# The first frequency step's rows written straight into its tile, two lead pieces, stores from ScalarE's queue

## The chip, the cores and the metric

The kernel runs on one core of a Trainium2 chip. The metric is device time in microseconds of one execution. Before the change three runs gave 1628.64 us in the median (1623.98 to 1630.26).

## The reference

The reference is a long causal convolution followed by a mixture of experts. Cut to what matters:

```python
# x, v: (4, 11456, 128); pos_emb: (11456, 64); w1: (64, 64); w2: (64, 128)
h_filt = (np.maximum(pos_emb @ w1, 0.0) @ w2) * np.exp(-0.01 * pos)[:, None]
u = x * v
Uf, Hf = np.fft.rfft(u, n=2 * S, axis=1), np.fft.rfft(h_filt, n=2 * S, axis=0)
y = np.fft.irfft(Uf * Hf[None], n=2 * S, axis=1)[:, :S]
x = (x * y).reshape(4 * 11456, 128)          # input of the second part

do_compute = x @ w_skip > 0
xc = x[do_compute]
logits = xc @ w_gate                          # 8 experts
e_idx = np.argmax(logits, axis=1)
gate_w = softmax(logits).max(-1)
y[m] = gate_w[m, None] * (np.maximum(xc[m] @ w1[e], 0.0) @ w2[e])   # m: tokens of expert e, F = 1024
out[do_compute] = xc + y
```

## The kernel before

The sequence is cut into `NB` = 3 blocks of 3840 positions, and each block is transformed in two stages, 60 x 64: a first transform over `K1` = 60 (matrix `c1`), and a second over `N2` = 64 with the twiddles folded in (`c2`, one 128x128 matrix for each of the 60 frequencies k). The 128 channels are handled in `NP` = 4 quarters of `DH` = 32.

**First phase** (`first_phase`, class `First`). For the first quarter it takes 16 data steps. A step loads 768 KB of x and v (`load`, L178, on SP's queue), multiplies them on VectorE (`mult`, L185), and transforms them in `Q` = 2 pieces: TensorE into PSUM (L202), ScalarE from PSUM to the buffer `xs` (L204), of which there are `XS` = 4. The result of a step has 120 partitions, (frequency k, real or imaginary c), and is stored to a DRAM tensor `x1d[0]` (`store`, L190, SP's queue), after the first piece of the next step. Between the pieces a generator, `filt`, computes the filter: 12 pieces of `post` (loaded on POOL's queue, L232; matmul L240; ReLU on ScalarE, L241), then 8 chunks x 3 blocks of L267 (TensorE), L268 (VectorE), L248 (TensorE) and L250 (ScalarE, into `fx`), and after each chunk two stores to the DRAM tensor `x1f` from POOL's queue (L256). `x1f` holds the filter for all quarters.

**Frequency phase** (`freq_phase`). It has 60 steps n: quarter h = n // 15, and `KS` = 4 of the 60 frequencies. `load(n)` issues on SP's queue, in this order: for h = 0 the matrices `c2` (L359), the data rows from `x1d[h]` (L362) and the filter's columns from `x1f` (L363) into a tile `x1` of [128, 4, 480], 384 columns of data and 96 of filter. The partition of `x1` is (c, n2), so a row of the first stage, which lies in one partition (k, c) for all n2, has to be spread over 64 partitions. That is what the trip through DRAM does. There are `QX` = 4 tiles `x1`, and three are loaded ahead. A step then does: L373 on TensorE (second transform into PSUM `xp`), L376 to L378 on ScalarE and L385 and L386 on VectorE (filter into `g`), L393 on VectorE (products `y`, `p1`, `p2`), L465 and L466 on POOL (sums), L404 on TensorE (transform back) with L405 on ScalarE, and the store to `zd` (L414, SP's queue). The PSUM pool `qps` for L404 and L202 has four buffers.

The data steps of the other three quarters, 48 in all, run inside the frequency phase: a generator `others()` yields after each half step, and `step()` takes two of these pieces whenever a credit allows. The first `LEAD` = 6 pieces (three data steps) are taken before the first frequency step is begun, and their products are on VectorE; later ones are on POOL.

After the last step the output phase (`out_phase`) transforms back over 60 and runs the experts.

The order of the instructions on each engine and queue is written out by hand: both phases stand under `manual_schedule`, so each engine's instructions and each queue's transfers go out in program order.

## Time and profile before

The profiled execution took 1626.78 us; its span is 1625.0 us (first to last instruction of the core), and its mean granted TensorE clock was 0.976.

| stage | from, to (us) | PE busy | ACT busy | DVE busy | POOL busy | share of the DMA engines |
|---|---|---|---|---|---|---|
| first phase, start | 0 to 40 | 28.92 | 15.93 | 6.77 | 6.88 | 0.80 |
| first phase, rest | 40 to 119 | 72.86 | 44.26 | 24.45 | 8.36 | 0.95 |
| between the phases | 119 to 143 | 8.96 | 5.16 | 2.88 | 0.00 | 0.75 |
| frequency phase with data steps | 160 to 568 | 407.65 | 204.21 | 324.92 | 354.43 | 0.97 |
| whole span | 1625.0 | 1537.8 | 794.3 | 1203.4 | 1084.8 | |

How to read the lines below: L202 is line 202 of the kernel. PE is TensorE's matmuls, PEld its weight loads, DVE VectorE, ACT ScalarE, POOL GpSimd, SP the engine that issues most transfers; a "q" behind a name (ACTq, SPq) is that engine's instruction queue, where a transfer's issue is shown with the time that the issue took, not the transfer. In a group's line stand the count, the busy time, the mean ns of one, the idle time of the engine before it and what ended that.

### The profile page before, as it was taken

How to read it: one execution, taken by the hardware profiler on the slowest of the kernel's cores; microseconds unless marked ns; L12 is line 12 of the kernel's file. 1: busy time of each engine (PE TensorE's matmuls, PEld its weight loads, DVE VectorE, ACT ScalarE, POOL GpSimd, SP SyncE). 2: the span in 40 equal slices, each digit the busy share in tenths (PEclk: the TensorE clock that was granted, in tenths of full speed). 3: DMA queues.
4: the chain of work that ended last, by engine and by line, in shares of the span. 5: the costliest groups of instructions: out<-in, count | busy, mean ns of one | idle time of the engine just before them, and what ended most of it. 6: DMA issues, size and time to landing. Idle time of an engine off the chain costs nothing.

```text
span 1625.0 us, 26505 instructions
## 1 busy us (share of the span) xinstructions
PE 1537.8 (95%) x8272; PEld 961.0 (59%) x8272; DVE 1203.4 (74%) x2424; ACT 794.3 (49%) x1677; POOL 1084.8 (67%) x850
## 2 busy tenths in 40 slices
PE   7985999999999999996789999999989999999997
PEld 2552444444444444442347766666767888888997
DVE  1324877888788799993877777777887777777886
ACT  4552455444544544442235544544345655556774
POOL 1112988888888878870156647855677888867885
PEclk9996999999999999997889999999999999999999
DMA  7998999999999799968978768877631111111110
GB/s 283 333 339 315 379 377 377 356 329 335 321 343 338 255 265 316 312 160 295 301 222 255 229 214 257 255 223 240 209 87 33 47 45 47 45 37 37 38 36 23
DMA packets 198532, 361.92 MB, mean 223 GB/s; under 512 B 64650, under 2 KB 138778, under 8 KB 198350
## 3 DMA queue, kind: packets, MB, share of 16 engines
q1 hardware_dynamic: 181078, 320.12, 58.9%
q0 software_dynamic: 16704, 38.89, 8.5%
q8 instruction: 67, 1.10, 0.3%
q10 hardware_dynamic: 608, 1.20, 0.2%
q14 instruction: 75, 0.61, 0.1%
HBM read 216.96 MB, written 145.69 MB: 223 GB/s over the span
## 4 chain that ended last, share of the span: by engine, by line
PE 84%; DMA 6%; DVE 5%; issue 3%; POOL 1%; ACT 1%; SPq 0%; DVEq 0%; ACTq 0%; POOLq 0%
PE ps L404 20%; PE xp L373 12%; PE bank L782 6%; PE y L1018 5%; PE ps L202 5%; PE my L834 4%; PE my L832 4%; PE hp L700 4%; PE my L833 4%; PE hp L702 4%; PE hp L701 4%; PE mh L700 2%; PE tp L1031 2%; PE mh L702 1%; PE mh L701 1%
## 5 line engine op out<-in xcount | busy, mean ns | idle before, releaser
L404 PE MATMUL ps<-y,c 128*128 128x512 f32 x720 | 331.3, 597 | 0.3
L465 POOL TENSOR_TENSOR y<-y,p 128x2048 f32<-128x2048 f32 x59 | 267.7, 4537 | 68.8 <-DVE p L393 68.8
L706 POOL DMA_INDIRECT out<-o,ids x186 | 199.9, 1075 | 123.3 <-DVE o L713 87.0
L404 PEld LDWEIGHTS ps<-y,c 128*128 128x128 f32 x720 | 133.4, 190 | 173.0 <-issue 155.9
L637 POOL DMA_INDIRECT xt<-out,ids x186 | 193.1, 1038 | 49.3 <-issue 30.6
L393 DVE TENSOR_TENSOR p<-xp,g 128x1024 f32<-128x1024 f32 x240 | 217.4, 947 | 0.0
L393 DVE TENSOR_TENSOR y<-xp,g 128x1536 f32<-128x1536 f32 x120 | 210.8, 1757 | 4.1
L821 DVE SCALAR_TENSOR_TENSOR hh<-hp,hh 128x1024 fp32r<-128x1024 f32 x130 | 158.4, 1219 | 68.3 <-ACT hh L820 68.1
L405 ACT COPY z<-ps 128x512 f32<-128x512 f32 x180 | 105.6, 586 | 176.5 <-PE ps L404 167.5
L820 ACT ACTIVATE hh<-hp 128x1024 fp32r<-128x1024 f32 x130 | 134.2, 1032 | 75.4 <-PE hp L702 75.4
L589 POOL DMA_INDIRECT lists<-pl,lies x32 | 53.6, 1676 | 141.0 <-DVE step L1116 72.3
L466 POOL TENSOR_TENSOR y<-y,p 128x1024 f32<-128x1024 f32 x59 | 139.0, 2356 | 4.6
L677 DVE TENSOR_TENSOR ws<-wf,ws 128x1024 fp32r<-128x1024 f32 x104 | 126.7, 1219 | 15.5 <-ACT ws L672 12.1
L610 POOL MEMSET idle<- 128x512 f16 x248 | 134.6, 543 | 0.2
L1018 PE MATMUL y<-zt,c 128*64 128x512 f32 x384 | 114.1, 653 | 19.8 <-DMA zt<-zd 11.2
L700 PE MATMUL hp<-hl,ws 128*128 128x512 f32 (+1 forms) x344 | 123.3, 359 | 3.5 <-DVE tb L626 1.9
L202 PE MATMUL ps<-wf,c 60*120 60x384 f32 x512 | 111.8, 532 | 14.8 <-DVE wf L185 14.3
L782 PEld LDWEIGHTS bank<-wd,h 128*128 128x128 f32 x896 | 104.2, 191 | 31.5 <-issue 31.4
L373 PE MATMUL xp<-x,wf 128*128 128x480 f32 x256 | 115.5, 575 | 7.3 <-issue 3.6
L204 ACT COPY wf<-ps 120x384 f32<-120x384 f32 x256 | 105.5, 493 | 29.5 <-PE ps L202 28.9
L702 PE MATMUL hp<-hl,ws 128*128 128x512 f32 (+1 forms) x344 | 116.4, 338 | 0.0
L834 PE MATMUL my<-hh,ws 128*128 128x512 f32 (+1 forms) x344 | 116.3, 338 | 0.0
(162 smaller groups left out, 3062.1 us busy)
## 6 DMA issues: line engine op xcount, KB each, us to landing
wf<-xv SPq DMA_DIRECT2D x64, 768.0 KB
zt<-zd SPq DMA_DIRECT2D x64, 768.0 KB
x1d<-wf SPq DMA_DIRECT2D x64, 720.0 KB
x<-x1d SPq DMA_DIRECT2D x60, 768.0 KB
zd<-z SPq DMA_DIRECT2D x118, 384.0 KB
out<-xm SPq DMA_DIRECT2D x96, 258.0 KB
ox<-xo SPq DMA_DIRECT2D x96, 256.0 KB
x1f<-fx POOLq DMA_DIRECT2D x16, 720.0 KB
```

Source lines behind the costliest of these rows:

```text
L202: nc.tensor.matmul(ps[p], self.c1[rows], u[rows, q * RUN:(q + 1) * RUN], start=True, stop=True)
L373: nc.tensor.matmul(xp[:, k, 0:(NS + NB) * DH], c2(n % PER * KS + j * KH + k), x1[:, j * KH + k], start=True, stop=True)
L393: nc.vector.tensor_tensor(o[:, :, :, j * KH:(j + 1) * KH].rearrange("p s a k b d -> p (s a) k b d"), x[:, None].broadcast_to([128, m, KH, ...
L404: nc.tensor.matmul(zps, c3[:, a, :], y[:, blk, a], start=(a == 0), stop=(a == 1))
L465: nc.gpsimd.tensor_tensor(y[:, 1:], y[:, 1:], p1, ALU.add)
L637: ins = nc.gpsimd.indirect_dma_start(out=xt[:, j], out_offset=None, in_=self.rows[0:have], in_offset=bass.IndirectOffsetOnAxis(ap=ids[:, j ...
L700: nc.tensor.matmul(hp, w[:, 0, c], hl[:, 0], start=True, stop=False)
L702: nc.tensor.matmul(hp, w[:, 1, c], hl[:, 0], start=False, stop=True)
L706: ins = nc.gpsimd.indirect_dma_start(out=self.rows, out_offset=bass.IndirectOffsetOnAxis(ap=ids[:, j:j + 1], axis=0), in_=o, in_offset=Non ...
L782: nc.tensor.matmul(bank[:, j * D:(j + 1) * D], h[f][:, j * 128:(j + 1) * 128], wd[s][:, f * D:(f + 1) * D], start=(f == 0), stop=(f == F / ...
L834: nc.tensor.matmul(y, w2[:, 1, c], h[:, 0], start=False, stop=(f == F // 128 - 1))
L1018: nc.tensor.matmul(y[p * 64:(p + 1) * 64], c4s[ch // C4][:, ch % C4, p, :], z[:, NP * p:NP * (p + 1)], start=True, stop=True)
```

## The change

- `First` takes the pool of the `x1` tiles and allocates one tile at once, `head`. A new function `direct` copies rows of the first stage from their SBUF partition to the partitions (c, n2) of `head`: for each of the 4 frequencies of the first step and each c one transfer of four rows. `data` calls it in every step of the first quarter (rows of 384 columns, 1.5 KB), `filt` for both halves of each chunk (rows of 96 columns, 384 B), all on ScalarE's queue. `load(0)` returns `head` and reads nothing from `x1d` and `x1f`.
- The first 8 of the 120 partitions are no longer stored to `x1d[0]`, so that store has 112 partitions. The `x1f` store is cut into 112 and 8 partitions.
- `store` issues on ScalarE's queue, at the end of the step itself.
- `LEAD` goes from 6 to 2: one data step is taken ahead of the first frequency step, and its product alone is on VectorE.
- The loads of x and v for later data steps are held back in the first phase (17 in place of 19 are issued there) and go out behind the loads for frequency step 1.
- `post` is loaded from SP's queue, one more piece ahead, and each load is issued behind the matmul of its turn.
- The credit of `step()` is spread over one more iteration. The pool of the `x1` tiles is opened earlier and closed after the frequency phase.

```diff
--- before.py
+++ after.py
@@ -42,7 +44,7 @@
 SOON = 4
 NKNOWN = sum(n * u for c, n, u in KNOWN)
 NEARLY = sum(n * u for c, n, u in KNOWN[:SOON])
-LEAD = 6
+LEAD = 2
 FLEAD = 2
 FEND = 2
 KS = 4
@@ -151,8 +153,9 @@
     ALL = NP * STEPS
     XV, US, XS = 3, 2, 4
 
-    def __init__(self, nc, i, x1d, x1f, mc, stage):
+    def __init__(self, nc, i, x1d, x1f, mc, stage, qx):
         self.nc, self.i, self.x1d, self.x1f = nc, i, x1d, x1f
+        self.qx, self.head = qx, self.tile(qx)
         n = self.Q * self.RUN
         at = [0]
 
@@ -167,9 +170,20 @@
         nc.sync.dma_start(self.c1, i["c1"])
         self.loaded, self.late = 0, []
 
-    def ahead(self, step):
-
-        while self.loaded < min(step + self.XV, self.ALL):
+    @staticmethod
+    def tile(qx):
+        return qx.tile([128, KS, (NS + NB) * DH], F32, name="x1")
+
+    def direct(self, eng, xs, n, cols):
+
+        for k in range(KS):
+            for c in range(2):
+                at = c * N2 + n
+                eng.dma_start(self.head[at:at + xs.shape[1], k, cols], xs[2 * k + c:2 * k + c + 1])
+
+    def ahead(self, step, most=XV):
+
+        while self.loaded < min(step + most, self.ALL if step >= self.STEPS else self.STEPS + LEAD // self.Q):
             self.load(self.loaded)
             self.loaded += 1
 
@@ -187,7 +201,7 @@
     def store(self):
 
         for dst, xs in self.late:
-            self.nc.sync.dma_start(dst, xs)
+            self.nc.scalar.dma_start(dst, xs)
         self.late = []
 
     def data(self, step, pool):
@@ -202,13 +216,14 @@
                 nc.tensor.matmul(ps[p], self.c1[rows], u[rows, q * RUN:(q + 1) * RUN], start=True, stop=True)
             for p in range(2):
                 nc.scalar.copy(xs[:, 2 * q + p], ps[p])
-            if q == 0:
-                self.store()
             if q < Q - 1:
                 yield
-        self.late.append((self.x1d[h][:, :, 2 * Q * ch:2 * Q * (ch + 1)].rearrange("k c m w -> (k c) m w"), xs))
-        if ch == self.STEPS - 1:
-            self.store()
+        n = 2 * Q * ch
+        at = KS if h == 0 else 0
+        if h == 0:
+            self.direct(nc.scalar, xs, n, slice(0, RUN))
+        self.late.append((self.x1d[h][at:, :, n:n + 2 * Q].rearrange("k c m w -> (k c) m w"), xs[2 * at:]))
+        self.store()
         yield
 
     def filt(self, fc, fp, pool):
@@ -229,15 +244,17 @@
         def positions(blk, k):
 
             pt = fp.tile([128, P], F32, name="post", bufs=4)
-            nc.gpsimd.dma_start(pt, i["post"][blk, k // P])
+            nc.sync.dma_start(pt, i["post"][blk, k // P])
             return pt
-        posts = [positions(*pc) for pc in pieces[:3]]
+        posts = [positions(*pc) for pc in pieces[:2]]
+        yield
+        posts += [positions(*pc) for pc in pieces[2:4]]
         yield
         for n, (blk, k) in enumerate(pieces):
-            if n + 3 < len(pieces):
-                posts.append(positions(*pieces[n + 3]))
             ps = pool.tile([128, P], F32, name="fa")
             nc.tensor.matmul(ps, w1, posts.pop(0), start=True, stop=True)
+            if n + 4 < len(pieces):
+                posts.append(positions(*pieces[n + 4]))
             nc.scalar.activation(hs[blk][:, k:k + P], ps, AF.Relu)
             yield
 
@@ -253,8 +270,12 @@
                 return
             for p in range(2):
                 n0 = p * H2 + ch * M
-                nc.gpsimd.dma_start(self.x1f[:, :, n0:n0 + M].rearrange("k c m w -> (k c) (m w)"),
-                                    xs[p].rearrange("k m h s d -> k (m h s d)"))
+                w = NB * DH
+                self.direct(nc.scalar, xs[p].rearrange("k m h s d -> k m (h s d)")[:, :, 0:w], n0, slice(self.RUN, self.RUN + w))
+                there = self.x1f[:, :, n0:n0 + M].rearrange("k c m w -> (k c) (m w)")
+                here = xs[p].rearrange("k m h s d -> k (m h s d)")
+                for rows in (slice(0, 112), slice(112, 2 * K1)):
+                    nc.gpsimd.dma_start(there[rows], here[rows])
         last = iter(())
         for ch in range(H2 // M):
             xs = [fp.tile([2 * K1, M, NP, NB, DH], F32, name=f"fx{p}") for p in range(2)]
@@ -285,6 +306,8 @@
         left = 0.0
         pieces = NB * 64 * H2 // 512 + 2 * NB * H2 // 4
         pace = (pieces - FLEAD) / (fi.Q * (fi.STEPS - FEND))
+        next(f)
+        fi.ahead(0, 1)
         next(f)
         fi.ahead(0)
         fi.mult(0)
@@ -318,7 +341,6 @@
         tc.manual_schedule(),
         tc.tile_pool(name="qc", bufs=1, reuse_waits="tile") as qc,
         tc.tile_pool(name="qp", bufs=2, reuse_waits="tile") as qp,
-        tc.tile_pool(name="qx", bufs=QX, reuse_waits="tile") as qx,
         tc.tile_pool(name="qpx", bufs=1, space=PSUM, reuse_waits="tile") as qpx,
         tc.tile_pool(name="qps", bufs=4, space=PSUM, reuse_waits="tile") as qps,
     ):
@@ -344,7 +366,7 @@
         def step():
 
             n = fi.STEPS * fi.Q
-            credit[0] += (n - LEAD) / (PER - QX) if done[0] < n else n / PER
+            credit[0] += (n - LEAD) / (PER - QX + 1) if done[0] < n else n / PER
             while credit[0] >= fi.Q:
                 credit[0] -= fi.Q
                 for _ in range(fi.Q):
@@ -357,7 +379,9 @@
             ks = slice(KS * k, KS * k + KS)
             if h == 0:
                 nc.sync.dma_start(c2(ks.start, KS), i["c2"][k])
-            x1 = qx.tile([128, KS, (NS + NB) * DH], F32, name="x1")
+            if n == 0:
+                return fi.head
+            x1 = fi.tile(fi.qx)
             w = NB * DH
             nc.sync.dma_start(x1[:, :, 0:fi.RUN], fi.x1d[h][ks].rearrange("k c n w -> (c n) k w"))
             nc.sync.dma_start(x1[:, :, fi.RUN:], fi.x1f[ks, :, :, h * w:(h + 1) * w].rearrange("k c n w -> (c n) k w"))
@@ -418,7 +442,11 @@
         done_z = []
         todo = others()
         ys = {}
-        xs = {n: load(n) for n in range(QX - 1)}
+        xs = {}
+        for n in range(QX - 1):
+            xs[n] = load(n)
+            if n == 1:
+                fi.ahead(fi.STEPS)
         for _ in range(LEAD):
             next(todo)
         gs, xps = {}, {}
@@ -1276,11 +1304,12 @@
     x1f = nc.dram_tensor("x1f", (K1, 2, N2, NB * D), F32).ap()
     zd = nc.dram_tensor("zd", (2, NP, H2 * 2 * K1 + ZR, NS * DH), F32).ap()
     lists = nc.dram_tensor("lists", (ROOM // PL, PL), I32).ap()
-    with tc.tile_pool(name="mc", bufs=1) as mc:
+    with tc.tile_pool(name="mc", bufs=1) as mc, ExitStack() as stack:
         wf = mc.tile([128, 2 * E * F], F32, name="wf")
-        fi = First(nc, i, x1d, x1f, mc, wf)
+        c3 = mc.tile([128, 2, 128], F32, name="c3")
+        qx = stack.enter_context(tc.tile_pool(name="qx", bufs=QX, reuse_waits="tile"))
+        fi = First(nc, i, x1d, x1f, mc, wf, qx)
         spare = wf[:, fi.used:]
-        c3 = mc.tile([128, 2, 128], F32, name="c3")
         first_phase(tc, fi)
         nc.scalar.dma_start(c3, i["c3"])
         nc.scalar.dma_start(zd.rearrange("p h r w -> (p h) r w")[:, H2 * 2 * K1:], i["none"])
@@ -1301,6 +1330,7 @@
                     yield
                 later["ex"].weights(e, 1)
         freq_phase(tc, nc, i, fi, zd, c3, spare, prepare())
+        stack.close()
         out_phase(tc, i, out, zd, later["ex"], later["consts"])
 
 
```

More of the change, by code (lines that the diff above doesn't have):

```diff
@@ L1 @@
+from contextlib import ExitStack
 import numpy as np
```

## The prediction

> **What bounds the kernel now.** I read the stages first, then the chain of waits where two of them meet, because the change acts there. The chain between the first phase and the frequency phase, in order of time (start, us, what):
>
> ```profile
> 115.44 1.30 ACT wf L204 x3
> ...
> 118.83 18.50 DMA x1d<-wf
> ...
> 137.35 0.39 SPq L362
> ...
> 138.06 4.58 DMA x<-x1f
> ...
> 142.78 2.74 PE xp L373 x3
> ```
>
> The first phase's last copy out of PSUM ends near 117, its last x1d store goes out at 118.83, and TensorE gets the first frequency step's rows at 142.78. So 24.0 us pass between that store and the first matmul of L373: 18.5 for the store to land, some for the issues, 4.6 for the load. The stages around it (busy us of each engine, granted clock, share of the DMA engines, GB/s):
>
> ```profile
> 40.00:119.00 79.00, 72.86 (x524) 42.84 (x520) 24.45 (x32) 44.26 (x96) 8.36 (x16) 0.98 0.95 335
> 119.00:143.00 24.00, 8.96 (x25) 3.88 (x26) 2.88 (x3) 5.16 (x12) 0.00 (x0) 0.51 0.75 259
> ...
> 160.00:568.00 408.00, 407.65 (x1144) 177.91 (x1143) 324.92 (x399) 204.21 (x531) 354.43 (x125) 1.00 0.97 341
> ```
>
> The columns after the length are PE, PEld, DVE, ACT, POOL. In the first phase the DMA engines are 95% busy and PE 92% (72.86 of 79); ACT works 44.26 of 79, a little over half. Between 119 and 143 PE does 8.96 us, at a clock of 0.51: this is the hole. From 160 on PE is never idle, so whatever work lands there costs its full time. All of the change lies before about 165 us or in the data steps of that last stretch.
>
> **The change part by part.**
>
> *The hole.* With the first step's rows written straight into its tile, its matmuls wait for the last of these writes, not for the round trip through DRAM. The nearest row for a small transfer from issue to release is this (chain of waits, 1 KB):
>
> ```profile
> 809.70 3.71 DMA ids<-lists
> ```
>
> So the first L373 would come 3.7 us after the last issue, in place of 24.0 us: 20.3 us is the most that can be won here, if the first phase ends when it did.
>
> *The direct writes.* They are many. `direct` issues KS x 2 = 8 transfers a call. `data` calls it in each of 16 steps (128), the filter for both halves of 8 chunks (128): 256 transfers of 6 KB or 1.5 KB, four rows each, all on ScalarE's queue. Does issuing occupy ScalarE? The timeline's first microseconds show it:
>
> ```profile
> 0.75 0.42 ACTq L224 DMA_DIRECT2D fw<-w  x1
> ...
> 1.20 0.46 ACTq L225 DMA_DIRECT2D win<-win  x1
> ...
> 1.68 0.45 ACTq L1285 DMA_DIRECT2D c<-c  x1
> 2.17 1.25 ACTq L1286 DMA_DIRECT2D zd<-none  x1
> 3.45 1.28 ACT L241 ACT_TABLE_LOAD   x1 [3.45 <-issue]
> ...
> 8.69 0.60 ACT L241 ACTIVATE h<-fa 128x512 f32<-128x512 f32 x1 [3.96 <-PE fa L240]
> ```
>
> The table load depends on nothing, yet starts at 3.45, just behind the fourth issue (2.17 + 1.25 = 3.42). An issue therefore stands in line with ScalarE's copies and takes 0.42 us or more here. Cheaper ones are on SP's queue, for small tables:
>
> ```profile
> 600.46 0.30 SPq L500 DMA_DIRECT2D shift<-shift  x1
> 600.81 0.29 SPq L502 DMA_DIRECT2D bump<-bump  x1
> 601.14 0.32 SPq L506 DMA_DIRECT2D sums<-sums  x1
> 601.50 0.32 SPq L508 DMA_DIRECT2D runs<-runs  x1
> 601.87 0.25 SPq L510 DMA_DIRECT2D lines<-lines  x1
> ```
>
> From one start to the next are 0.33 to 0.37 us. A write of four rows on ScalarE's queue isn't in the trace. Its lower bound is 0.25 us, the shortest issue above; its upper bound is 0.58, from the only other ScalarE issues:
>
> ```profile
> 731.69 1.16 ACTq L414 DMA_DIRECT2D zd<-z  x2
> ```
>
> I take 0.33, the start-to-start time of `bump`, whose eight rows are nearest to four: 256 x 0.33 = 84.5 us (64 to 148).
>
> What this is added to is ScalarE's own work up to 119 us (line, busy us, idle before):
>
> ```profile
> L204 ACT COPY wf<-ps 120x384 f32<-120x384 f32 x64 | 27.5, 495 | 10.7 <-PE ps L202 10.7
> L250 ACT COPY fx<-ps 120x512 f32<-120x512 f32 x48 | 26.8, 592 | 28.1 <-PE ps L248 14.8 <-DMA x1f<-fx 11.9 <-PE fa L267 1.3
> L241 ACT ACTIVATE h<-fa 128x512 f32<-128x512 f32 x12 | 7.2, 597 | 14.7 <-PE fa L240 14.7
> ```
>
> 61.5 us of copies, against 110 us from its first one at 8.69 to 119. There is room for some 49 us of issues, and I count 84.5. So ScalarE becomes the bound of the first phase.
>
> A rule speaks the other way. The Trainium skill, "DMA: Bandwidth & Descriptors", section "Issuing engines are not separate DMA queues", holds that issue time is usually small beside the transfer itself; by it the 84.5 would drop out of the sum and the forecast would turn into the first rival's time. Here 6 KB at the 335 GB/s of the first-phase row is 0.02 us, and the 0.33 issue is the longer of the two; the trace does not bear the rule out for such pieces.
>
> *The x1d stores on ScalarE's queue.* SP's price is
>
> ```profile
> L190 SPq DMA_DIRECT2D x1d<-wf x64: 317/388/2376, 16.8 to 565.3; - x64
> ```
>
> (minimum, median, maximum ns). In the first phase 16 x 0.39 = 6.2 us more on ScalarE. In the frequency phase 48 of them join a ScalarE that is busy 204.21 of 408 us: at the median 18.7 us, at the maximum 114 us, both less than its idle time. I cost them at 0; what covers them is the four PSUM buffers between PE and the copies. On SP they freed the loads behind them, which waited long:
>
> ```profile
> SPq L190 <- ACT wf L204: 80.2, 15, 10.9
> ...
> SPq L178 <- DMA fw<-w: 0.8, 1, 0.8
> ```
>
> (80.2 us in the first 142 us, in 15 waits.) I credit nothing for that: xv loads come sooner, but ScalarE sets the pace.
>
> *Idle time of ScalarE.* The second row above is an xv load that waits for a weight transfer whose bytes it doesn't touch; in the frequency phase there is the like:
>
> ```profile
> SPq L359 <- DMA zd<-z: 2.3, 6, 0.5
> ```
>
> A c2 load shares nothing with a zd store. I read it as a small set of completion slots given out in turn, so a burst of 16 writes (5.3 us) may wait for its own first ones to land (3.7). Besides, ScalarE waited 10.7 + 14.7 us for PE in L204 and L241, part of it at the start for `post`. Bounds 0 and 25 us; I take 12.
>
> *End of the first phase.* 8.7 (first copy) + 61.5 + 84.5 + 6.2 + 12 = 172.9, then 3.7 to land: first L373 at 176.6 in place of 142.78, **+33.8**. The lead step's copies lie inside the 3.7.
>
> *The second frequency step* still goes through DRAM. Its rows are wanted when L373 starts on it, in the profile at
>
> ```profile
> 151.69 1.85 PE L373 MATMUL xp<-x,wf 128*128 128x480 f32 x4 [3.56 <-issue]
> ```
>
> 8.9 us after the first, so at 185.5. The last store leaves at 172.9, lands some 4 us later with the DMA engines no longer full (the same traffic over 173 us), and its load takes the 4.6 of the chain: 182. Cost 0; if the store needed 18.5 as before, 10 us more.
>
> *Two lead pieces in place of six* (each piece is half a data step): two data steps leave the hole, where PE was idle, for the stretch where it isn't. Its pace:
>
> ```profile
> 186.78 3.43 PE ps L404 x8
> 196.88 3.43 PE ps L404 x8
> 208.90 3.43 PE ps L404 x8
> ```
>
> 10.10 us an iteration with one data step, 12.02 with two, so 1.92 each: 2 x 1.92 = **+3.8**. POOL takes over their products; it works 354.43 of 408 there, so 3.6 us more (1.82 each) fits.
>
> *The rest.* Twelve `post` loads move to SP's queue (0.35 each on a queue that mostly waits), x1f is stored in two parts (POOL's DMA issues, 8.36 us of 79, double under a longer phase), two xv loads come later: 0 each.
>
> Sum: +33.8 + 3.8 = +37.6 on the profiled execution's own 1626.8 (span 1625.0 and 1.8 around it), 1664. That execution lies 1.9 under the median of the runs, less than the price of an issue is uncertain by.
>
> **The rivals.**
>
> 1. *ScalarE's issues fit into its idle time: faster.* The place is the first phase, the price that of one issue, and the point is where (142.78 - 3.7 - 3.8 - 8.7 - 61.5 - 6.2) / 256 = 0.23 us with no idle at all. Below that the hole closes. No issue in the rows above is that short. The second step's rows would then be late: the last store at 118.8 and 19 to 24 us for its trip (two xv loads fewer in front: 1.57 MB at 335 GB/s is 4.7 us), so 138 to 143 in place of 151.69: -9 to -14, +3.8: about 1619.
>
> 2. *Four engines.* The writes might crowd on few of the 16 DMA engines: 128 x 6 KB + 128 x 1.5 KB = 0.98 MB; on four of them 0.25 MB each, at 335 / 16 = 20.9 GB/s 11.8 us more in a phase that is 95% full. With cheap issues the first phase ends at 130.6, the first L373 at 134.3, -8.5 + 3.8: 1622. With issues at 0.33 it hides under ScalarE. The same page of the Trainium skill, section "Why a DMA increments its semaphore by 16 and not by 1", says just this: a transfer whose outer size is four runs on the lowest four engines. No row here splits the engines.
>
> 3. *A dear issue.* At the 0.58 of `zd<-z`, 64 us more: 1728.
>
> 4. *ScalarE late in the frequency phase.* If the store waits there for a slot or a full queue (the 2.4 us maximum) ahead of the copies PE needs, 48 times, and half a microsecond of each shows: +24 on the forecast, 1688. For it: PE has no slack. Against: half of ScalarE's time there is free.
>
> 5. *It doesn't do what it says.* The round trip only moves to the second step, and what is won goes back: within 0.5%, about 1628. Against: that step has 8.9 us of cover.
>
> **How the numbers follow.** Forecast (ScalarE bounds the first phase, issue 0.28 to 0.42, idle 0 to 25): 0.60, 1640 to 1698. Rival 1: 0.13. Rival 2: 0.03. Rival 3: 0.10. Rival 4: 0.07. Rival 5: 0.07. What can be told from no change here is about 0.5%, 8 us. Faster 0.16, same 0.07, slower 0.77. The forecast's own range leaves too much out, so it is widened to 1626 and 1712: below lies rivals 1 and 2, above half of rival 3.
>
> **What would show it.** Right: in the first phase ACT with its queue is busy nearly without a gap, PE and DMA shares fall (DMA to about 0.65), the first L373 comes near 177, the hole after the last copy is some 4 us. Wrong: direct writes start less than 0.23 us apart, or the first L373 comes before 142 us. Each issue's start-to-start time, the start of L373, and the iterations of 12.02 us (two more of them) test the three terms separately.

## The result and the profile after

The changed kernel took 1760.81 us in the median of its runs (1759.29 to 1765.65), the kernel before 1628.72 beside them: a ratio of 1.0829, with a 95% interval of 1.081 to 1.0849. (Ratios here and below are estimates over all the runs with their intervals; they differ by up to 0.24% from the quotient of the two medians, here 1.0811.) The forecast was 1664, in a range of 1626 to 1712. The direction was right; the loss is 132 us where 37.6 was forecast.

The profiled execution took 1759.29 us (span 1757.5). Where the stages meet, the chain of waits now reads like this (start, us, what):

```profile
255.27 0.59 ACTq L182
255.85 0.04 issue
255.89 0.59 ACTq L182
256.48 0.04 issue
256.52 0.59 ACTq L182
...
266.86 0.59 ACTq L182
267.48 4.00 DMA x1d<-wf
271.57 0.39 SPq L386
...
272.13 6.67 DMA x<-x1f
...
278.94 3.23 PE xp L397 x4
```

L182 is the issue of a direct write. The writes themselves are the chain: 0.59 us each and 0.04 to the next, so 0.62 to 0.63 from start to start (0.626 as the mean of a burst of eight, which takes 5.01). Behind the last one comes the round trip through DRAM that the change took from the first frequency step; the second step now waits for it (4.00 to land, 6.67 to load).

The prices of the issues, from the views by tile (minimum, median and maximum ns, then first and last start):

```profile
L182 ACTq DMA_DIRECT2D x<-wf x128: 587/587/1657, 15.6 to 266.9; - x128
L182 ACTq DMA_DIRECT2D x<-fx x128: 587/587/1867, 54.9 to 253.7; - x128
L204 ACTq DMA_DIRECT2D x1d<-wf x64: 314/323/715, 20.7 to 705.9; - x64
L397 PE MATMUL xp<-x,wf x256: 566/566/1137, 265.0 to 791.5; 128*128 128x480 f32 x128
```

The first matmul of the frequency phase (L397, formerly L373) starts at 265.0 in place of 142.78. ScalarE's timeline shows what stands around the writes:

```profile
80.59 5.01 ACTq L182 DMA_DIRECT2D x<-wf  x8
85.64 0.45 ACTq L204 DMA_DIRECT2D x1d<-wf  x1
86.13 1.07 ACT L267 COPY fx<-ps 120x512 f32<-120x512 f32 x2 [5.57 <-DMA x<-wf]
86.75 12.59 ACTq L182 DMA_DIRECT2D x<-fx  x16
99.38 0.86 ACT L218 COPY wf<-ps 120x384 f32<-120x384 f32 x2 [12.18 <-DMA x<-fx]
```

Eight writes of a data step take 5.01 us, the sixteen of a filter chunk 12.59, which is 2.6 more than 16 x 0.626. The copies out of PSUM stand behind them. The time that ScalarE's copies stood behind writes, issues and all, up to 280 us (total, times, longest):

```profile
ACT fx L267 <- DMA x<-fx: 72.4, 5, 18.6
ACT fx L267 <- DMA x<-wf: 50.0, 9, 5.6
ACT wf L218 <- DMA x<-fx: 23.2, 2, 12.2
ACT wf L218 <- DMA x<-wf: 16.7, 3, 5.6
```

And the stages (length, then PE, PEld, DVE, ACT, POOL, granted clock, share of the DMA engines, GB/s):

```profile
40.00:119.00 79.00, 40.85 (x236) 22.73 (x232) 11.24 (x15) 16.85 (x36) 6.54 (x12) 0.78 0.45 153
119.00:265.00 146.00, 66.93 (x320) 40.25 (x320) 14.45 (x19) 30.20 (x64) 12.64 (x22) 0.65 0.40 130
...
290.00:698.00 408.00, 407.28 (x1146) 177.59 (x1143) 322.26 (x397) 207.23 (x533) 351.87 (x124) 1.00 0.98 344
```

The first phase went from a stage with full DMA engines (0.95) and a busy PE (72.86 of 79) to one in which PE and the DMA engines idle about half of the time, and DVE and POOL more, while ScalarE's queue issues. The frequency phase is what it was: 407.28 of 408 us.

The whole difference lies before the end of the frequency phase. Its first matmul comes 122.3 us later (142.78 to 265.04). The stretch from there to the start of the last matmul of the transform back is 9.7 us longer: 587.6 us before (142.8 to 730.4) and 597.3 after (265.0 to 862.3), by the views of that line, before and after:

```profile
L404 PE MATMUL ps<-y,c x720: 592/592/697, 157.4 to 730.4; 128*128 128x512 f32 x180
L428 PE MATMUL ps<-y,c x720: 592/592/697, 285.3 to 862.3; 128*128 128x512 f32 x180
```

Together that is 132.0 of the 132.5 us between the two profiled executions.

### The profile page after: what moved, and what is told of

Read it like the earlier page. It is cut to its first block, busy times and chain, and to the rows that moved or that the text cites. A ratio compares the mean times of both kernels' runs of the same rounds, so it can differ in the third digit from the quotient of the medians.

```text
span 1757.5 us, 26788 instructions
## 1 busy us (share of the span) xinstructions
PE 1565.8 (89%) x8272; PEld 977.3 (56%) x8272; DVE 1200.9 (68%) x2422; ACT 795.6 (45%) x1677; POOL 1090.7 (62%) x856
## 4 chain that ended last, share of the span: by engine, by line
PE 74%; ACTq 7%; DMA 7%; DVE 6%; issue 2%; ACT 2%; DVEq 0%; POOL 0%; SPq 0%; POOLq 0%
PE ps L428 17%; PE xp L397 10%; ACTq L182 7%; PE bank L810 5%; PE y L1046 5%; PE ps L216 4%; PE my L862 3%; PE my L860 3%; PE hp L728 3%; PE my L861 3%; PE hp L730 3%; PE hp L729 3%; PE mh L728 2%; PE tp L1059 2%; DMA zd<-z 1%
## 5 line engine op out<-in xcount | busy, mean ns | idle before, releaser
L216 PE MATMUL ps<-wf,c 60*120 60x384 f32 x512 | 125.1, 563 | 39.0 <-ACT wf L218 33.3
L278 POOL DMA_DIRECT2D x1f<-fx x32 | 17.1, 542 | 226.5 <-ACT fx L267 226.5
L289 DVE TENSOR_TENSOR hw<-fa,win 128x512 f32<-128x512 f32 x24 | 16.6, 692 | 174.9 <-PE fa L288 174.9
L218 ACT COPY wf<-ps 120x384 f32<-120x384 f32 x256 | 106.5, 494 | 59.1 <-DMA x<-fx 23.2
L728 PE MATMUL hp<-hl,ws 128*128 128x512 f32 (+1 forms) x344 | 123.3, 359 | 3.5 <-DVE tb L654 1.9
L397 PE MATMUL xp<-x,wf 128*128 128x480 f32 x256 | 116.6, 580 | 9.5 <-DMA x<-x1f 8.9
```

The costliest lines, as they stand in the source:

```text
L216: nc.tensor.matmul(ps[p], self.c1[rows], u[rows, q * RUN:(q + 1) * RUN], start=True, stop=True)
L397: nc.tensor.matmul(xp[:, k, 0:(NS + NB) * DH], c2(n % PER * KS + j * KH + k), x1[:, j * KH + k], start=True, stop=True)
L728: nc.tensor.matmul(hp, w[:, 0, c], hl[:, 0], start=True, stop=False)
```

## The experiments

The theory after the result: the direct writes cost the time, as issues that stand in ScalarE's order of work, at 0.63 us each. The rivals: the writes are slow only in this form; it is not the issue but the wait for earlier transfers to land; and the other edits of the change take a part. The table gives the start of the first xp matmul in the profiled execution, the median and the ratio to the kernel before with its 95% interval; the runs are told one by one below it. The start is that of one execution, and the executions of some versions lie far apart (e1 1636.9 to 1650.59 us, e6 1631.6 to 1649.03), so a few microseconds of it between two versions show nothing.

| run | edit | first xp | median us | ratio |
|---|---|---|---|---|
| (changed kernel) | | 265.0 | 1760.81 | 1.0829 [1.081, 1.0849] |
| e1_via_dram | no direct writes, all other edits | 149.1 | 1643.37 | 1.0111 [1.0076, 1.0146] |
| e3_data_only | data's 128 writes only | 187.7 | 1681.82 | 1.0333 [1.0297, 1.0368] |
| e2_sp_pool | data's on SP, filter's on POOL | 181.2 | 1673.03 | 1.0274 [1.0245, 1.0304] |
| e4_four_rows | source of four partitions | 255.9 | 1748.49 | 1.0742 [1.0705, 1.0779] |
| e5_to_dram | 256 writes, but into DRAM | 231.5 | 1728.09 | 1.0609 [1.0553, 1.0666] |
| e7_data_sp | data's 128 only, on SP | 174.4 | 1660.71 | 1.0191 [1.0161, 1.0221] |
| e8_last_steps | 32 writes, last four data steps | 152.7 | 1651.39 | 1.0147 [1.0111, 1.0183] |
| e15_only_direct | the writes alone, no other edit | 284.9 | 1765.34 | 1.0851 [1.0825, 1.0878] |
| e6_lead6 | e1 with six lead pieces | 161.5 | 1643.29 | 1.0079 [1.0052, 1.0106] |
| e9_stores_sp | e6, stores back on SP | 154.3 | 1644.55 | 1.0084 [1.0057, 1.011] |
| e10_posts_pool | e6, `post` back on POOL | 160.6 | 1645.59 | 1.0088 [1.0062, 1.0114] |
| e12_one_store | e6, x1f stored whole | 147.4 | 1641.97 | 1.0061 [1.0039, 1.0082] |
| e13_three_back | no writes, all of these back | 144.3 | 1626.98 | 1.0004 [0.9991, 1.0018] |
| e14_order_back | e13, xv order back | 144.0 | 1627.26 | 1.001 [0.9993, 1.0027] |
| e16_credit | e13, the change's rate of data steps | 142.4 | 1628.3 | 0.9988 [0.9969, 1.0008] |
| e17_stores_act | e13, stores on ScalarE's queue | 145.3 | 1635.37 | 1.0027 [1.0008, 1.0047] |
| e18_posts_sp | e13, `post` on SP's queue | 143.4 | 1635.86 | 1.0031 [1.0011, 1.0051] |
| e11_lead2 | kernel before with two lead pieces | 144.5 | 1637.08 | 1.0017 [0.9991, 1.0044] |

**Without the writes, and with half of them.** `e1_via_dram` stores all rows to `x1d` and `x1f` and loads the first step from there like any other:

```diff
-        at = KS if h == 0 else 0
-        if h == 0:
-            self.direct(nc.scalar, xs, n, slice(0, RUN))
+        at = 0
...
-                self.direct(nc.scalar, xs[p].rearrange(...)[:, :, 0:w], n0, slice(self.RUN, self.RUN + w))
...
-            if n == 0:
-                return fi.head
-            x1 = fi.tile(fi.qx)
+            x1 = fi.head if n == 0 else fi.tile(fi.qx)
```

> The changed kernel without the direct writes: the first step's rows go through DRAM again (x1d store of 120 rows, loads for step 0), everything else of the change stays (stores on ScalarE's queue, post on SP's queue, x1f in two parts, two lead pieces). Theory A (the 256 issues at 0.63 us in ScalarE's stream are the loss): the first L397-like matmul comes at 138 to 147 as before, total 1622 to 1638 (before plus some 4 for the two data steps that now run in the frequency phase, less what earlier xv loads win). Rival C (stores on ScalarE's queue and the fewer lead pieces cost a large part): 1660 or more.

117.4 us come back, 89% of the loss. But 1643.37 is above the expected 1638: the other edits cost something too, which is taken up below. `e3_data_only` leaves out the filter's writes alone (the second deletion above; `load(0)` then reads the columns of the filter, and not those of the data):

> The changed kernel with the 128 data writes on ScalarE's queue; the filter's columns of step 0 are read from x1f through DRAM, so its 128 writes are gone. Theory A (a price per issue): 128 x 0.63 = 80 us and about half of the waits less, some 5 back for the x1f trip: first phase ends at 170 to 180, total 1665 to 1685. Rival B (the bytes on few DMA engines; the filter's writes are a fifth of them): 1725 to 1740.

1681.82, as theory A had it. The two runs give the price of a write twice. The last 128 of 256 cost 1760.81 - 1681.82 = 79.0 us, 0.617 each, close to the 0.626 of the chain: behind a full ScalarE an issue counts about whole. (Their bursts take 93.9 us in the profile, so part of the waits inside them was not lost.) The first 128 cost 1681.82 - 1643.37 = 38.5, 0.30 each. At 0.626 they are 80.1 us of issues, so 41.6 us of these were hidden, near the 49 us of room on ScalarE that the forecast counted.

**On other queues.** `e2_sp_pool` changes `nc.scalar` in the two calls of `direct`, to `nc.sync` for the data and `nc.gpsimd` for the filter.

> The changed kernel, same 256 writes of the same bytes, but the 128 of data issued from SP's queue and the 128 of the filter from POOL's. Theory A (ScalarE's stream): ScalarE's copies run as before, SP carries 128 x 0.63 = 80 us of issues and POOL 160 x 0.54 = 86 us, both below 120; first phase ends between 120 and 145, first matmul of the frequency phase by 150, total 1610 to 1645. Rival B (the writes themselves are slow to land, on few DMA engines or for want of completion slots, whichever queue issues them): the first phase stays above 200 us, total 1700 or more.

Neither: 1673.03. ScalarE is free of the writes, but they do not become cheap. The views by tile, and the waits of POOL up to 190 us:

```profile
L182 SPq DMA_DIRECT2D x<-wf x128: 572/573/2687, 15.7 to 181.0; - x128
L182 POOL DMA_DIRECT2D x<-fx x128: 518/518/709, 47.8 to 177.7; - x128
```

```profile
POOL x L182 <- DMA x1f<-fx: 37.0, 17, 5.4
```

An issue costs 0.57 us on SP and 0.52 on POOL. And on POOL the writes waited 37.0 us for x1f stores on the same queue, which write other bytes. `e7_data_sp` is e3 with its 128 writes on SP's queue:

> e3_data_only with its 128 data writes issued from SP's queue in place of ScalarE's; the filter's columns of step 0 through DRAM. Theory A (ScalarE's stream is the bound, the writes as such are cheap): the first phase ends at 118 to 130, the first frequency matmul comes at 130 to 148, total 1622 to 1645. Rival B (each write has to wait for an earlier one to land, 1.0 to 1.3 us apiece as on SP's queue in e2): the data writes take 140 to 165 us, first frequency matmul at 155 to 175, total 1650 to 1670.

1660.71, the rival's range: 21 us better than on ScalarE, 17 worse than none. Its bursts of eight, in SP's timeline, took about twice what they take on ScalarE, with xv loads between them:

```profile
65.73 8.74 SPq L182 DMA_DIRECT2D x<-wf  x8
75.56 11.25 SPq L182 DMA_DIRECT2D x<-wf  x8
88.49 10.54 SPq L182 DMA_DIRECT2D x<-wf  x8
```

**What makes an issue dear.** `e4_four_rows` asks whether it is the shape, one partition spread over four. The source becomes four partitions of the buffer, so the tile then holds other rows:

```diff
-                eng.dma_start(self.head[at:at + xs.shape[1], k, cols], xs[2 * k + c:2 * k + c + 1])
+                eng.dma_start(self.head[at:at + xs.shape[1], k, cols], xs[4 * (2 * k + c):4 * (2 * k + c) + 4, 0])
```

> The changed kernel, same 256 writes with the same bytes on ScalarE's queue, but each reads its four rows from four partitions in place of one; so the head tile holds other rows than it should, and step 0 computes from those. Theory A1 (an issue on ScalarE's queue costs this much whatever its shape): 0.59 us each, total 1750 to 1765. Theory A2 (the price belongs to a source of one partition spread over four): 0.30 to 0.36 us each as the x1d stores there, 256 x 0.26 = 67 us less: 1685 to 1700.

The issue takes 592 ns in place of 587: the shape is not it. The kernel takes 1748.49, just under A1's 1750 and far from A2; why it is 12 us faster than the changed kernel at the same issue was not taken apart. `e5_to_dram` takes e1 and adds 256 writes from such four rows on ScalarE's queue, but into a DRAM tensor that nothing reads, so they are work beside the computation:

```diff
-                at = c * N2 + n
-                eng.dma_start(self.head[at:at + xs.shape[1], k, cols], xs[2 * k + c:2 * k + c + 1])
+                to = self.junk[self.put][:, 0:cols.stop - cols.start]
+                eng.dma_start(to, xs[4 * (2 * k + c):4 * (2 * k + c) + 4, 0])
+                self.put += 1
```

> e1_via_dram (step 0 through DRAM) with 256 extra writes on ScalarE's queue at the places of the direct ones, each four rows of the same length, but into a DRAM tensor that nobody reads. If the dear issue belongs to a destination in SBUF, an issue takes 0.30 to 0.35 us here, ScalarE gets 256 x 0.36 = 92 us more against some 45 of idle time, first phase ends near 175, total 1680 to 1705. If any four-row write on ScalarE's queue costs 0.59, the end of the first phase is that of the changed kernel and the trip through DRAM comes on top: 1755 to 1775.

The issue is cheap, by the view by tile:

```profile
L183 ACTq DMA_DIRECT2D junk<-wf x128: 246/307/1776, 16.7 to 219.3; - x128
L183 ACTq DMA_DIRECT2D junk<-fx x128: 246/307/2214, 47.6 to 211.0; - x128
```

0.31 against 0.59 for the same four rows on the same queue: for these writes the price goes with the destination, SBUF or DRAM. (Not for all: the zd stores of the forecast's bound, 0.58, go into DRAM. What makes those dear was not tried.) Yet 1728.09 is over the expected 1705. The timeline of ScalarE shows why:

```profile
118.63 0.92 ACTq L206 DMA_DIRECT2D x1d<-wf  x1
119.59 9.32 ACTq L183 DMA_DIRECT2D junk<-fx  x16
129.02 1.07 ACT L269 COPY fx<-ps 120x512 f32<-120x512 f32 x2 [14.92 <-DMA junk<-fx]
...
133.58 2.68 ACTq L183 DMA_DIRECT2D junk<-wf  x8
```

One burst of eight writes takes 2.68 us, 0.33 each; one of sixteen takes 9.32, 0.58 each, and the longest single issue took 2.214 against a median of 0.307. So there is a second price: the writes of a long burst take longer than their issues at the median. That they wait there for earlier transfers to land fits, but no run isolates it. With both prices 256 writes pushed the first xp matmul from 149.1 to 231.5.

**Few and late writes.** If the first writes are hidden in idle time, a version might write only the last four data steps' rows directly (32 writes, half on SP's queue and half on ScalarE's), since only those are late for the round trip. `e8_last_steps` does that, with two lead pieces before the first frequency step and four behind it:

```diff
-        if h == 0:
-            self.direct(nc.scalar, xs, n, slice(0, RUN))
+        if h == 0 and ch >= self.STEPS - LATE:
+            self.direct((nc.sync, nc.scalar), xs, n, slice(0, RUN))
...
-                eng.dma_start(self.head[at:at + xs.shape[1], k, cols], xs[2 * k + c:2 * k + c + 1])
+                eng[c].dma_start(self.head[at:at + xs.shape[1], k, cols], xs[2 * k + c:2 * k + c + 1])
```

> The changed kernel, but only the last four data steps of the first quarter write directly (32 writes, half on SP's queue, half on ScalarE's); the rows of the other twelve and the filter's columns of step 0 come through DRAM, their loads behind the last write; the filter ends two data steps earlier; two data steps run between the first and second frequency step. Theory: 16 issues on ScalarE fit into its idle time, first frequency matmul at 125 to 135, the second step then waits for the trip of the last stores to about 142: 8 us less than before, 1614 to 1624. Rival (the loads for step 0 wait behind the stores all the same): 1625 to 1640.

Missed, above the rival's range too: 1651.39, 8 us worse than e1, with the first xp matmul at 152.7. Four writes on ScalarE's queue took up to 7.13 us:

```profile
116.97 6.01 ACTq L183 DMA_DIRECT2D x<-wf  x4
129.78 3.87 ACTq L183 DMA_DIRECT2D x<-wf  x4
136.00 7.13 ACTq L183 DMA_DIRECT2D x<-wf  x4
```

At the median of 0.630 us here, four would take 2.5. The DMA engines' share was 0.98 from 110 to 119 us and 0.82 from 119 to 143. The copies stood 17.6 us behind these writes.

**The writes alone.** `e15_only_direct` is the kernel before with the direct writes and nothing else: six lead pieces, stores on SP's queue, `post` on POOL's, x1f stored whole.

> The kernel before with the 256 direct writes alone (first step not loaded, stores of the data without the first four frequencies, on SyncE's queue; six lead pieces). Theory: the writes stand for nearly all of the loss, and what they cost adds to the rest: 117 us on 1628.7, so 1738 to 1752 us, with the writes 0.62 to 0.64 us apart. Rival: the writes cost less without the stores beside them on ScalarE's queue: under 1730 us.

Above both: 1765.34, a ratio of 1.0851. So the writes alone account for the whole loss; whether the other edits beside them cost or win anything in total is below what the overlapping intervals tell. The profiles share it out differently: without the other edits the last write leaves at 279.1 in place of 267.5, and the first matmul, behind three lead steps, comes at 284.9 in place of 265.0; but the stretch behind it takes 587.8 us in place of 597.3. In the stores' queue, SP's, the waits up to 285 us are

```profile
SPq L204 <- DMA x<-fx: 138.0, 8, 19.2
SPq L204 <- ACT wf L218: 67.4, 17, 8.1
SPq L204 <- DMA x<-wf: 34.7, 7, 6.1
```

An x1d store shares no bytes with a write of the filter's columns, and is on another queue, but waits for it 138 us, by the profile. That fits the forecast's reading that transfers take turns with a small set of completion slots, here one that SP's and ScalarE's queues would share; the POOL row above is the like within one queue. No run isolated that reading.

**The other edits.** Without writes they cost 16 us against the kernel before's 1627.38 beside it (e1). The first suspect was the two lead pieces. `e6_lead6` is e1 with `LEAD = 6`:

> e1_via_dram with six lead pieces again in place of two. Theory: of the 16 us that e1 lost against before, the two data steps in the frequency phase are 4 and the rest is PE's hole that nothing fills, so six lead pieces give most of it back: 1627 to 1635. Rival (the stores on ScalarE's queue, the post loads and the x1f parts on other queues cost it): stays at 1638 to 1646.

1643.29, no gain: the rival. But the profiles show what the lead is worth: from the first xp matmul to the last matmul of the transform back e1 takes 592.3 us, e6 587.5. Two lead steps moved out cost 4.8 us there. That e6 is no faster in total goes with a later first matmul in its profile (161.5 for 149.1), and that profile is one of its longest executions (1648.42).

From e6 three runs each put one edit back: the x1d stores on SP's queue; the `post` loads on POOL's queue, three ahead; one whole x1f store for the two of 112 and 8 rows.

> The kernel without direct writes and with six lead pieces (it took 1643.29 us, 1.0079 of the kernel before, its first xp matmul at 161.5 us), with one more part undone: the x1d stores are issued from SyncE's queue again, at the place where the kernel before issues them. Theory S, the stores on ScalarE are what the rest of the change costs (23 stores of 0.32 us stand before ScalarE's copies, and copies wait 9.3 us for x1d stores to land): 1626 to 1633 us, first xp matmul at 143 to 150 us. Rival F, the cost is at the filter's stores to x1f (ScalarE's copies waited 29.5 us for them there, 11.9 in the kernel before): no gain, 1638 to 1647 us, first xp matmul after 157 us.

> The kernel without direct writes and with six lead pieces (1643.29 us), with the loads of post issued from GpSimd's queue again, three ahead as in the kernel before; stores stay on ScalarE's queue and x1f is stored in two parts. Theory P, the 24 loads on SyncE's queue delay the loads of xv: 1626 to 1633 us. Rival F, the filter's stores to x1f cost it: no gain, 1638 to 1650 us, and ScalarE's copies still wait over 20 us for x1f stores to land.

> The kernel without direct writes and with six lead pieces (1643.29 us), with each half piece of x1f stored whole (120 rows) by one transfer from GpSimd's queue, as in the kernel before, and not by one of 112 rows and one of 8. Theory F, the split stores are what the rest of the change costs (32 issues of 0.54 us and 29.5 us of ScalarE waiting for x1f to land, against 16 issues and 11.9 us before): 1626 to 1635 us, first xp matmul at 143 to 152 us. Rivals S and P (stores on ScalarE's queue, post on SyncE's queue): 1638 to 1647 us, first xp matmul after 157 us.

1644.55, 1645.59, 1641.97: theories S, P and F all fall, as single causes. The rival F missed two of its signs as well: e9's first matmul came at 154.3, not after 157, and in e10 ScalarE's copies waited 17.9 us for x1f stores, not over 20. (The loads of `post` are 12, not the 24 of that expectation.) Theory F had the start of the first matmul right (147.4) and the time wrong. The group of that matmul (busy us, mean ns, idle before it) in e12:

```profile
L390 PE MATMUL xp<-x,wf 128*128 128x480 f32 x256 | 118.0, 586 | 17.9 <-DMA x<-x1f 15.1 <-issue 2.6
```

TensorE stood 15.1 us before the first of these matmuls, for x1f's columns. With all edits back but the place of the `x1` tiles and the order of the xv loads (`e13_three_back`), that wait is 3.7:

```profile
L389 PE MATMUL xp<-x,wf 128*128 128x480 f32 x256 | 117.6, 584 | 6.8 <-DMA x<-x1f 3.7 <-issue 3.2
```

> No direct writes, and stores, loads of post, the whole x1f stores and the lead of six pieces all as in the kernel before: of the change only the new place of the x1 tiles in SBUF and the new order of the xv and x loads around the end of the first phase stay. Theory D, several small delays that each cover for the other (undoing one alone gave 1642 to 1646): 1627 to 1633 us. Rival O, the order of the xv and x loads or the place of the tiles costs it: 1637 to 1646 us, with TensorE waiting over 10 us at the second frequency step.

> As the run before it, with the xv loads in the order of the kernel before too: only the place of the x1 tiles in SBUF is the change's. Theory D and rival O both: 1626 to 1631 us, the time of the kernel before. If it stays over 1635 us, where the tiles lie costs the time.

1626.98 and 1627.26, the kernel before's time. The place of the tiles and the order of the loads cost nothing. The two waits do not explain e12's time, though: its first matmul comes only 3.1 us behind e13's (147.4 and 144.3), because in e13 a lead step fills the time. Of the 12.7 us between the two profiled spans, 3.1 lie before the first matmul, -0.9 in the stretch to the last transform back (588.2 and 589.1) and 10.5 behind it (902.0 and 891.5), in the output phase, which no edit here touches. Over the profiles of all the runs that last part takes between 891.2 and 902.0 us. So one profile can't show where a version that is some 5 us slower loses its time.

But e13 had also put back the rate at which the frequency phase takes data steps, which the three runs before it had not, so that could be a single cause after all. `e16_credit` gives e13 the change's rate again (`PER - QX + 1`); `e17_stores_act` and `e18_posts_sp` give it one edit each, the stores and the `post` loads.

> The version of 1626.98 us (no direct writes; stores, post, whole x1f stores and six lead pieces as in the kernel before) with the change's rate of data steps in the frequency phase, credit over PER - QX + 1 in place of PER - QX. In the three runs that each undid one edit this rate had stayed the change's, so it could be the one cause of their 10 to 16 us. Theory R, the rate is the cause: 1636 to 1645 us. Theory D, several edits that cover for each other: 1625 to 1631 us.

> The version of 1626.98 us with the x1d stores alone moved to ScalarE's queue as the change has them. Theory D (any two of the edits give nearly the whole cost, one alone gives part of it or all): 1631 to 1642 us. Theory R: 1625 to 1631 us.

> The version of 1626.98 us with the loads of post alone moved to SyncE's queue as the change has them (two, then one load of xv, then two, then four ahead). Theory D: 1631 to 1642 us. Theory R: 1625 to 1631 us.

The rate costs nothing (0.9988); theory R falls. The stores alone cost 0.27%, `post` alone 0.31%, some 4 to 5 us each, and both together (e12) 0.61%, about the sum. Each of them with the split stores gave 0.88% and 0.84% (e10, e9), so by subtraction the split is worth some 0.5 to 0.6%; it was not run alone. All three together gave 0.79% (e6), less than the 1.1 to 1.2 of the sum. If that holds, a third edit adds little to two others, and this is why undoing one won nothing. It is not shown: the intervals are 0.2 to 0.3% to each side, the ratios come from different sets of runs, and the gap between sum and e6 is not clear of them. In the group of the first matmuls of e17 stands a wait of 14.7 us for a c2 matrix, a load on SP's queue that has no bytes of a store:

```profile
L386 PE MATMUL xp<-x,wf 128*128 128x480 f32 x256 | 115.7, 576 | 18.5 <-DMA wf<-c 14.7 <-issue 3.8
```

That wait is not the stores' cost: the first matmul comes at 145.3, 1.0 us behind e13's. Where the 4 to 5 us are lost stays open.

`e11_lead2` is the kernel before with `LEAD = 2`:

> The kernel before with two lead pieces and nothing else changed. By the forecast's term for the moved data steps (two steps of 1.92 us of TensorE): 1632 us, 1630 to 1634; the first xp matmul up to 4 us earlier and the end of the frequency phase 2 to 6 us later. Rival: the lead pieces were cover for the first loads of x1f, so that moving them out changes nothing before the first xp matmul and everything later is as long or longer: 1634 to 1642 us.

1637.08; its interval, 0.9991 to 1.0044, holds the forecast's 3.8 us (1.0023) as well as no change. The profile bears out both in part. As the rival had it, the first matmul does not come earlier (144.5); before it stands

```profile
L373 PE MATMUL xp<-x,wf 128*128 128x480 f32 x256 | 117.7, 584 | 21.6 <-DMA x<-x1f 18.5 <-issue 2.9 <-PE ps L404 0.2
```

18.5 us of waiting for x1f's columns, where the kernel before waited 3.2:

```profile
142.78 5.35 PE L373 MATMUL xp<-x,wf 128*128 128x480 f32 x8 [3.16 <-DMA x<-x1f]
```

The lead pieces were cover for loads. And as the forecast's term had it, the stretch from there to the last matmul of the transform back is 4.5 us longer, 592.1 us (144.5 to 736.6) for 587.6:

```profile
L404 PE MATMUL ps<-y,c x720: 592/592/697, 159.9 to 736.6; 128*128 128x512 f32 x180
```

No version here is faster than the kernel before by more than its interval.

## Why the prediction missed

**The bound: right.** The forecast said that ScalarE becomes the bound of the first phase through the issues on its queue, that the DMA engines' share falls, and that the second frequency step still goes through DRAM. All three are in the profile after (the DMA engines' share at 0.45 and 0.40, lower than the 0.65 that was named), and e1 and e15 show that the writes cost the time.

**The step that failed is the term "256 x 0.33 = 84.5".** The sum of the first phase, term by term, with what the profile after has:

| term | forecast | measured | from |
|---|---|---|---|
| first ScalarE operation | 8.7 | 8.5 | its timeline |
| copies | 61.5 | 61.1 | groups of L218, L267, L258 up to 265 |
| direct writes | 84.5 | 179.7 | sum of the bursts, 85.8 data and 93.9 filter |
| x1d stores | 6.2 | 7 | 16 x about 0.45 |
| idle | 12 | 11 | what is left up to 267.5 |
| to the first matmul | +3.7 | -2.4 | 265.0: it needs only the first frequency's rows |
| first xp matmul | 176.6 | 265.0 | |

Of the 95 us by which the writes were undersized, 75.8 are the issue (256 x 0.626 = 160.3 for 84.5), and 19.4 are time in the bursts beyond that, above all in the filter's sixteens. The price was chosen by the number of rows, from loads on SP's queue out of DRAM; the row that the writes resembled was the upper bound, a slow issue of 0.58 (`zd<-z`), and it was named. e4 and e5 show that neither the rows nor the shape of the source decide, since four rows cost 0.59 into SBUF and 0.31 into DRAM. No row of the profile before had a transfer from SBUF into SBUF, so nothing there spoke for 0.33 more than for 0.58, and 0.60 against the 0.10 of the third rival was too sure.

**The third rival** (dear issue, 1728) had nearly the right price but not the rest: 0.626 from start to start for 0.58, the extra time in the bursts, and the second step. Those are 11.8 + 19.4 + 5.0; less the 6.1 by which the first matmul did not wait for the last write, they lead from 1728 to 1758, close to the 1759.29 of the profiled execution.

**The idle term was sized right by luck.** The 12 us were to cover waits for completion slots and for PE; the 11 that are left are short gaps between writes and copies, most of them waits for PE (12.4 us in the view of ScalarE's waits behind its first operation, part of that under issues), and the 19.4 in the bursts came on top. Even at the forecast's issue price the time would have been longer than forecast: in e5, at 0.31 an issue, the first matmul came at 231.5. That run's first step takes the trip through DRAM; taking off the 20.3 us at which the forecast put it still leaves, as an estimate, 211 and not 176.6.

**The Trainium skill's rule** ("DMA: Bandwidth & Descriptors", section "Issuing engines are not separate DMA queues"), that issue time is usually small beside the transfer, was weighed and rejected, and the runs bear the rejection out: 0.59 us an issue, and 79.0 us for 128 of them.

**The second step, costed at 0, cost 5.0.** From the first step's first matmul to the second's the profile has 13.90 us (265.04 to 278.94) for 8.91 before (142.78 to 151.69). The forecast had the store land in some 4 us, and it did (4.00); the whole trip took 11.5 us (267.48 to 278.94) where 9.1 was forecast, and its load 6.67 where 4.6 was. More of the loss is the cover: the first step was to begin 3.7 us after the last write had been issued, and it began 2.4 us before. The forecast's alternative ("10 us more", a store that needs 18.5) is not what happened. PE stood 8.94 us:

```profile
265.04 4.96 PE L397 MATMUL xp<-x,wf 128*128 128x480 f32 x8 [0.43 <-DMA x<-wf]
278.94 3.23 PE L397 MATMUL xp<-x,wf 128*128 128x480 f32 x4 [8.94 <-DMA x<-x1f]
```

**The two lead steps, +3.8: about right.** The stretch behind the first xp matmul grew by 9.7. Taking off the second step's 5.0 leaves 4.7. The same two steps cost 4.5 there in e11 and 4.8 between e6 and e1, each by one profile; over all profiles the stretch takes 587.5 to 589.7 us with six lead pieces, and 592.1 to 593.6 with two where the first step is read through DRAM (e1, e5, e11). So the forecast's own sum, with 265.0 for 176.6, 5.0 for 0 and 4.7 for 3.8, gives 1759, the time of the profiled execution: the writes are where it failed.

**The rest, 0 each**: "Twelve `post` loads", the x1f halves and the stores' queue. With the writes there they cost nothing that shows (e15, which has none of them, is no faster than the changed kernel), as is to be expected where ScalarE sets the pace. Without them the same edits cost 16 us (e1), and alone the stores' queue and `post`'s queue cost some 4 to 5 each (e17, e18). A cost of 0 held only under the bound that the forecast had named.

**The other rivals.** The first (cheap issues, 1619) fell with the price; so did the second, and no run splits the engines. The fourth, ScalarE late in the frequency phase, did not occur: PE 407.28 of 408 with the stores on ScalarE's queue at 323 ns. The fifth fell: the changed kernel is slower by 8%.

## What to carry to other kernels

The small transfers here are priced by the issue and not by the byte (0.59 us for 6 KB and for 1.5 KB), and the issue stands in line with the work of the engine on whose queue it is. Before many of them are put on an engine that also drains PSUM, multiply their number by a price measured for the same kind of source and destination, and add what a long burst of them takes beyond that. Moving them to another queue moved the price here, but did not remove it (e2, e7). An edit that wins nothing when it is undone alone is not yet free: add it alone to the version without the others, too.

## What the runs showed of the hardware that was not expected

- The same issue of four rows on ScalarE's queue took 587 to 592 ns into SBUF and 307 ns into DRAM; from SBUF into SBUF it took 573 on SP's queue and 518 on POOL's. An x1d store of 720 KB took hardly longer to issue (323 ns, e1) than a write of four rows into DRAM.
- By the profile, transfers wait for others that write other bytes: across queues, x1d stores on SP's 138.0 us for ScalarE's filter writes (e15); on one queue, POOL's writes 37.0 us for x1f stores (e2). Whether the chip or the program's own waits make them do so, no run isolated.
- With PE busy 66.93 of 146 us, the granted clock was 0.65 between 119 and 265 us; with PE busy 72.86 of 79, in the first phase of the kernel before (40 to 119), it was 0.98.
